# Attention and MoE block on one core: the layernorm's mean is subtracted from the data instead of from the output weights, scales are summed in one pass, and the list scheduler models the transfer queue

## The chip, the core and the metric

The kernel runs on one core of a Trainium2 chip. The metric is device time in microseconds; less is better. Every execution computes the whole result from tensors that lie in device memory. The profiler took one execution of the kernel before; all views quoted below are of that execution.

## What is computed

Eight batches of eight-head attention (576 tokens, head size 64), half of the heads with a local mask (the 32 latest keys), half with a strided mask (keys whose distance is a multiple of 32), then a feed-forward block over 4608 tokens:

```python
x = attention(q, k, v).transpose(0, 2, 1, 3).reshape(4608, 512)
h = x @ w_in                                  # 512 -> 1024
e = exp(h - max(h)); sm = e / (sum(e) + 1e-9)
solu = h * sm
mu = mean(solu); var = mean((solu - mu) ** 2)
ln = (solu - mu) / sqrt(var + 1e-6) * g_ln
out = ln @ w_out                              # 1024 -> 512
```

All tensors are float32, except that the two weight matrices are handed over as 64-bit numbers and decoded on the chip.

## The kernel before

**Precision by splitting.** [...] Each factor is scaled by a power of two and split into a high and a low half of 16 bits (`whi`/`wlo`, `xhi`/`xlo`, `c[:,0]`/`c[:,1]`, `ohi`/`olo`), and each product is three passes: high by high, high by low, low by high. The scales come from `pow2_scale`: a sum of squares over all partitions (on TensorE, line 254, a product with a matrix of ones, one 128x1 float32 product per column to add), whose exponent is halved on VectorE (L260 to L268).

**Attention.** A batch is five units (`UNITS`): two of the strided heads, three of the local heads. A unit runs query times key (L347 puts the mask into PSUM, L352 multiplies), the row maximum and the difference on VectorE (L358, L359), exp on ScalarE (L361), row sums (L362, L366, L367), the normalisation on GpSimd (L370), the 16-bit split (L376, L377), a transposing DMA (L379, tile `pt`), the product with the values (L400, into `x_ps`), and the split of the result into `xhi` and `xlo` (L416, L417). Before it `v_scale` and `v_split` (L289, L307, L308) prepare the values, and DMAs of L323 copy them into a second layout.

**Feed-forward.** 36 tiles of 128 tokens (`ff`, L421). The first product, here called g1, is two halves of 12 matrix products of 128x512 (L458 to L460), each half into one of three PSUM banks (`h_ps`). A tile uses two of them, so that the second half of the next tile has to wait until this tile's `h` was read for the last time (L469). Then, for a tile: maximum (L465) and its scaling (L466) on VectorE, exp with its sum (L467) on ScalarE, `u = h * e` with its sum (L469) and the mean (L472) on VectorE, the sum of squared deviations (L473) on ScalarE, six small instructions on GpSimd (L477 to L487) that end in the inverse root `r`, `c[:,0] = u * r` on ScalarE (L490), the low half `c[:,1]` on VectorE (L491), one transposing DMA (L494, tile `ct`, three buffers), the second product, here called g2 (24 products, L498 to L500), the scaling into `ob` on ScalarE (L506) and the store (L507). The mean itself is never subtracted from `u`: the mean over the rows of g times w_out is taken off the weights instead.

**Weights.** Both weight matrices are loaded in pieces of 128 rows and decoded (L522, L525, L528, L529). For `w_in`, ScalarE and TensorE make the two halves (L541, L547 to L557). For `w_out`, `prep_o` (L559) builds two gain matrices on GpSimd (L567, L570), sums the weighted rows on TensorE (L574, eight float32 products of 128x512) and squares on ScalarE (L562); `split_o` (L585) then forms, for each of the eight chunks, gain times weight minus the mean with two float32 products (L590, L591) in `x_ps`, and splits that (L594, L595). The two `x_ps` banks are those that the attention units use.

**What sets the order.** Nothing is ordered by hand. Each step is added to a `Plan` with an engine, an assumed duration, a key and the names that it reads and writes; `Plan.order` simulates the five engines with these durations, takes at each moment the ready step with the lowest key, and the instructions are then issued in that order. Each engine executes its own instructions strictly in this order. All loads, copies and transposes are issued by SyncE; the stores by ScalarE. In the plan a DMA takes 5 us beyond its turn in the queue (`DMA_LATENCY`), and SyncE may run 1 us ahead of it (`DMA_AHEAD`).

## Time and profile before

| what | value |
|---|---|
| runs | 567.52, 572.67, 572.97 us; median 572.67 |
| the profiled execution, first to last instruction | 566.9 us |
| lowest run less that span | 0.6 us |
| median less that span | 5.8 us |
| TensorE busy | 505.7 us, 89% of the span |
| VectorE, ScalarE, GpSimd busy | 355.9, 301.8, 156.7 us |
| mean granted TensorE clock | 0.985 |
| moved by DMA | 96.9 MB, mean 171 GB/s |

The profiled execution has no time of its own beside its span of 566.9 us; the sums of the prediction are made against that span, and the last step goes from it to the runs. Matrix products overlap, and each is shown with its full length: a product of 128x512 shows 0.38 us, but the next one starts 0.216 us later. What a step of TensorE costs is therefore read from the start of one step to the start of the next.

### The profile page before, as it was taken

To read this page: it belongs to the slowest core of one execution; us is meant where nothing else is said; L and a number is where in the kernel's file an instruction comes from. 1 tells how busy PE (TensorE), PEld (TensorE's weight loads), DVE (VectorE), ACT (ScalarE), POOL (GpSimd) and SP (SyncE) were. 2 spreads that over 40 slices of the span, in tenths; PEclk is the share of its full clock that TensorE was granted. 3 is DMA by queue.
4 is the path that set the end of the run, shared out by engine and by line. 5 is a ranking of instruction groups with operands and counts; after the bars stand their busy time and mean duration, and the time that the engine had idled before them with its cause. 6 is when DMAs were issued, how large, how long until landed. Compare 5 with 4: busy or idle time off the path is not lost.

```text
span 566.9 us, 11879 instructions
## 1 busy us (share of the span) xinstructions
PE 505.7 (89%) x4864; PEld 256.9 (45%) x4864; DVE 355.9 (63%) x633; ACT 301.8 (53%) x446; POOL 156.7 (28%) x309
## 2 busy tenths in 40 slices
PE   0348998999798999899999999999989999999986
PEld 0233444345453555455454554555545554444432
DVE  3596367867466775677766776877656777343430
ACT  3765824685256553755674556555744644345350
POOL 2320002433132342334331332322323323113130
PEclk9999978899999999999999999999999999999999
DMA  8999149629992999599938996899679635533332
GB/s 312 413 258 272 35 120 227 140 59 247 190 250 56 225 217 237 127 175 236 254 86 122 271 221 138 198 206 240 162 137 180 139 80 111 87 84 84 77 91 74
DMA packets 171158, 96.90 MB, mean 171 GB/s; under 512 B 138208, under 2 KB 157280, under 8 KB 171104
## 3 DMA queue, kind: packets, MB, share of 16 engines
q1 hardware_dynamic: 165920, 86.71, 70.8%
q10 hardware_dynamic: 5184, 9.44, 5.1%
q8 instruction: 38, 0.62, 0.5%
q14 instruction: 16, 0.13, 0.1%
HBM read 39.24 MB, written 9.44 MB: 86 GB/s over the span
## 4 chain that ended last, share of the span: by engine, by line
PE 72%; DVE 10%; DMA 9%; ACT 5%; issue 2%; POOL 1%; ACTq 0%; SPq 0%; DVEq 0%
PE h_ps L458 10%; PE h_ps L459 9%; PE h_ps L460 9%; PE o_ps L498 9%; PE o_ps L499 9%; PE o_ps L500 9%; PE x_ps L400 4%; PE s_ps L352 4%; DMA pt<-p 3%; DMA ct<-c 2%; DVE u L469 2%; DMA vrl<-vloc 2%; ACT e L467 2%; PE h_ps L553 2%; PE s_ps L347 1%
## 5 line engine op out<-in xcount | busy, mean ns | idle before, releaser
L458 PE MATMUL h_ps<-w,xhi 128*128 128x512 f16 x280 | 108.5, 388 | 10.5 <-DVE u L469 7.6
L459 PE MATMUL h_ps<-w,xhi 128*128 128x512 f16 x280 | 108.2, 386 | 0.0
L460 PE MATMUL h_ps<-w,xlo 128*128 128x512 f16 x280 | 107.7, 385 | 0.0
L498 PE MATMUL o_ps<-obuf,ct 128*128 128x512 f16 x272 | 103.4, 380 | 1.0 <-DMA ct<-c 0.8
L499 PE MATMUL o_ps<-obuf,ct 128*128 128x512 f16 x272 | 103.3, 380 | 0.0
L500 PE MATMUL o_ps<-obuf,ct 128*128 128x512 f16 x272 | 103.2, 379 | 0.0
L370 POOL TENSOR_TENSOR t<-t,m 128x576 f32<-128x576 f32 (+2 forms) x40 | 47.4, 1184 | 126.9 <-DVE m L367 101.1
L467 ACT ACTIVATE e<-h_ps,st,vsc 128x1024 f32<-128x1024 f32 x31 | 37.2, 1201 | 64.8 <-DVE st L466 49.4
L465 DVE TENSOR_REDUCE st<-h_ps 128x1 f32<-128x1024 f32 x35 | 42.6, 1218 | 41.9 <-PE h_ps L460 41.9
L477 POOL TENSOR_SCALAR st<-st 128x1 f32<-128x1 f32 x36 | 11.4, 316 | 208.3 <-DVE st L472 198.8
L469 DVE SCALAR_TENSOR_TENSOR u<-h_ps,e 128x1024 f32<-128x1024 f32 x35 | 42.8, 1222 | 29.1 <-ACT e L467 17.7
L473 ACT ACTIVATE e<-u,st 128x1024 f32<-128x1024 f32 x36 | 41.3, 1147 | 35.3 <-DVE st L472 32.1
L491 DVE SCALAR_TENSOR_TENSOR c<-u,st,c 128x1024 f16<-128x1024 f32 x36 | 47.0, 1304 | 14.6 <-ACT c L490 14.6
L417 DVE TENSOR_TENSOR xlo<-x_ps,xhi 128x384 f16<-128x384 f32 (+2 forms) x40 | 25.6, 641 | 40.4 <-ACT xhi L416 40.3
L490 ACT ACTIVATE c<-u,st 128x1024 f16<-128x1024 f32 x36 | 41.2, 1145 | 16.8 <-POOL st L487 16.0
L459 PEld LDWEIGHTS <-xhi 128*128 128x128 f16 x288 | 28.5, 99 | 40.2 <-issue 12.9
L498 PEld LDWEIGHTS <-ct 128*128 128x128 f16 x288 | 28.2, 98 | 39.4 <-DMA ct<-c 5.5
L458 PEld LDWEIGHTS <-xhi 128*128 128x128 f16 x288 | 28.8, 100 | 35.4 <-issue 5.9
L460 PEld LDWEIGHTS <-xlo 128*128 128x128 f16 x288 | 28.6, 99 | 35.4 <-issue 2.5
L500 PEld LDWEIGHTS <-ct 128*128 128x128 f16 x288 | 28.2, 98 | 34.2 <-issue 0.3
L499 PEld LDWEIGHTS <-ct 128*128 128x128 f16 x288 | 28.2, 98 | 32.3
L352 PE MATMUL s_ps<-k,q 64*54 64x54 f32 (+1 forms) x1280 | 41.8, 274 | 0.0
(143 smaller groups left out, 766.2 us busy)
## 6 DMA issues: line engine op xcount, KB each, us to landing
out<-ob ACTq DMA_DIRECT2D x36, 256.0 KB, 3.1
vrs<-vstr SPq DMA_DIRECT2D x8, 768.0 KB, 5.8
vd<-vs SPq DMA_DIRECT2D x16, 384.0 KB, 7.5
vrl<-vloc SPq DMA_DIRECT2D x8, 640.0 KB, 5.7
q<-qstr SPq DMA_DIRECT2D x8, 594.0 KB, 4.9
k<-kstr SPq DMA_DIRECT2D x8, 594.0 KB, 6.5
q<-qloc SPq DMA_DIRECT2D x8, 576.0 KB, 5.2
k<-kloc SPq DMA_DIRECT2D x8, 576.0 KB, 6.8
```

Of the source, the lines that this page charges most:

```text
L352: nc.tensor.matmul(s_ps[row : row + nq, pair, i * nk : (i + 1) * nk], q_raw[half][hs, q0 : q0 + (nq - 1) * nqb + 1 : nqb], k_raw[half][hs, ...
L370: add("pool", nx * nk / 500 + 0.1, lambda: nc.gpsimd.tensor_tensor(tv, tv, sm.unsqueeze(2).broadcast_to([P, nx, nk]), op=ALU.mult), key + ...
L458: nc.tensor.matmul(hv[:, i], xhi[:, cc, tok], whi[:, cc, cols], start=(cc == 0), stop=False)
L459: nc.tensor.matmul(hv[:, i], xhi[:, cc, tok], wlo[:, cc, cols], start=False, stop=False)
L460: nc.tensor.matmul(hv[:, i], xlo[:, cc, tok], whi[:, cc, cols], start=False, stop=(cc == 3))
L465: add("dve", 1.21, lambda: nc.vector.tensor_reduce(nm, hv, axis=AX.XY, op=ALU.max, negate=True), key + 0.2, r=HH, w=[(ST, "nm")])
L467: add("act", 1.3, lambda: nc.scalar.activation(ev, hv, AF.Exp, bias=nm, scale=hs, accum_out=z), key + 0.25, r=[*HH, (ST, "nm"), *SC], w=[E ...
L469: add("dve", 1.3, lambda: nc.vector.scalar_tensor_tensor(uv, hv, 1.0, ev, op0=ALU.mult, op1=ALU.mult, accum_out=us), key + 0.3, r=[*HH, E] ...
L491: add("dve", 1.35, lambda: nc.vector.scalar_tensor_tensor(c[:, 1], u, r, c[:, 0], op0=ALU.mult, op1=ALU.subtract), key + 0.45, r=[U, (ST, ...
L498: nc.tensor.matmul(o, ct[:, cc, :], ohi[:, cc, :], start=(cc == 0), stop=False)
L499: nc.tensor.matmul(o, ct[:, cc, :], olo[:, cc, :], start=False, stop=False)
L500: nc.tensor.matmul(o, ct[:, 8 + cc, :], ohi[:, cc, :], start=False, stop=(cc == 7))
```

## The change

1. **The mean.** The data is centred: ScalarE now makes `c[:,0] = u - mean` (with the mean as bias), VectorE the low half of it, and neither waits for the variance. The sum of squares (now into a scratch tile) comes after that, and GpSimd's five small instructions, which end in the factor `f` of the store, come last. The weights need no mean: `gmat`, `gdiag`, the eight products of L574, the sixteen of L590 and L591 and the copy `mt` are gone. `split_o` multiplies the decoded weight by gain times scale on ScalarE and takes the low half on VectorE, straight from SBUF; the decoded weights lie four chunks further up in `obuf`, so that the halves can be written below them.
2. **A range factor per tile.** Since `c` is no longer divided by the deviation, `u` is multiplied by a power of two `ia` that two small VectorE instructions (`span`) derive from the largest `h`; the scaling of the maximum is now three values wide.
3. **Scales.** `pow2_scale` adds its columns with one VectorE reduction into a 16-bit number and then runs one product with 16-bit ones, instead of one float32 product per column.
4. **The planner.** SyncE's transfers carry four numbers (how many queue entries, time to issue, delay until it begins, time to land), the queue is at most 100 entries deep, every landing is taken 3 us late, engines are free a little before a step ends, and most assumed durations are set anew. The base keys of the units, loads and tiles are unchanged.

The core of the diff, with long parts cut:

```diff
-    DMA_LATENCY = 5.0
-    DMA_AHEAD = 1.0
     HOP = 0.4
+    LATE = 3.0
+    DEEP = 100
+    SKIP = {"act": 0.1, "dve": 0.08, "pe": 0.07, "pool": -0.1}
...
-                dma_free = max(dma_free, now + 0.55) + dur
-                free[e] = max(now + 0.55, dma_free - self.DMA_AHEAD)
-                end = dma_free + self.DMA_LATENCY
+                pushes, issue, begins, lands = steps[n][6]
+                start = max(now + begins, dma_free)
+                dma_free = start + dur
+                pieces.append((start, dma_free, moved, moved + pushes))
+                moved += pushes
+                free[e] = now + issue + 0.06
+                for a, b, c, d in reversed(pieces):
+                    if c < moved - self.DEEP <= d:
+                        free[e] = max(free[e], a + (b - a) * (moved - self.DEEP - c) / (d - c))
+                        break
+                end = dma_free + lands + self.LATE
...
-        def total():
-            for i, part in enumerate(parts):
-                nc.tensor.matmul(tot, ones, part, start=(i == 0), stop=(i == len(parts) - 1))
+        def part_sum():
+            with nc.allow_low_precision(reason="a power of two is made of it"):
+                nc.vector.tensor_reduce(one, parts, axis=AX.X, op=ALU.add)
...
+        add("pe", 0.15, lambda: nc.tensor.matmul(tot, ones, one, start=True, stop=True), key, r=["ones", (w, "one")], w=[T])
...
+        def span():
+            nc.vector.tensor_scalar(near, up, floor, down, op0=ALU.max, op1=ALU.max)
+            nc.vector.tensor_scalar(ia.bitcast(I32), near.bitcast(I32), 0x7FFFFFFF, 0x7F800000, op0=ALU.bitwise_xor, op1=ALU.bitwise_and)
...
-        add("act", 1.35, lambda: nc.scalar.activation(e, u, AF.Square, bias=mean, scale=Q, accum_out=sq), key + 0.35,
-            r=[U, (ST, "mean")], w=[E, (ST, "sq")])
...
-        add("act", 1.2, lambda: nc.scalar.mul(c[:, 0], u, r), key + 0.4, r=[U, (ST, "r")], w=[(C, 0)])
-        add("dve", 1.35, lambda: nc.vector.scalar_tensor_tensor(c[:, 1], u, r, c[:, 0], op0=ALU.mult, op1=ALU.subtract), key + 0.45,
+        add("act", 1.2, lambda: nc.scalar.activation(c[:, 0], u, AF.Identity, bias=mean, scale=1.0), key + 0.35, r=[U, (ST, "mean")], w=[(C, 0)])
+        add("dve", 1.28, lambda: nc.vector.scalar_tensor_tensor(c[:, 1], u, mean, c[:, 0], op0=ALU.add, op1=ALU.subtract), key + 0.4,
...
+        add("act", 1.24, lambda: nc.scalar.activation(junk[:, 0:DF], u, AF.Square, bias=mean, scale=1.0, accum_out=sq), key + 0.42,
...
-        for cc in range(8):
-            add("pe", 0.87, lambda cc=cc: nc.tensor.matmul(o_ps, gmat[:, cc], obuf[:, cc], start=(cc == 0), stop=(cc == 7)), key,
-                r=["gmat", ("od", cc)], w=["o"])
...
-            def center(cc=cc, x=x):
-                nc.tensor.matmul(x, gdiag[:, cc], obuf[:, cc], start=True, stop=False)
-                nc.tensor.matmul(x, ones[0:1], mt_sb[0:1], start=False, stop=True)
...
+            add("act", 0.68, lambda cc=cc, go=go: nc.scalar.mul(ohi[:, cc], o32[:, cc], go), key, r=[("od", cc), "go"], w=[("oh", cc), *past])
```

What this does to the order shows at three places.

ScalarE near the end of the weight preparation, before: `ob` is the square of a `w_out` chunk, `xhi` the split of an attention unit, `junk` the squares of the next batch's values, and the `obuf` written from `x_ps` is the high half of a centred `w_out` chunk.

```order
L376 CAST p_97<-t_91 128x6x96
L562 ACTIVATE ob_113,o_sc_128<-obuf_126 128x512
L525 ACTIVATE obuf_126<-room_70 128x512
L562 ACTIVATE ob_113,o_sc_128<-obuf_126 128x512 x2
L416 CAST xhi_102<-x_ps 128x2x192
L525 ACTIVATE obuf_126<-room_67 128x512
L562 ACTIVATE ob_114,o_sc_128<-obuf_126 128x512 x2
L289 ACTIVATE junk_71,vm_79<-vrl_72 128x1280
L562 ACTIVATE ob_114,o_sc_128<-obuf_126 128x512
L289 ACTIVATE junk_71,vm_79<-vrs_73 128x1536
L583 COPY mt_122<-o_ps 128x512
L416 CAST xhi_102<-x_ps 128x2x192
```

And after the change, where `obuf` written from `obuf` with `gg` is the high half of a `w_out` chunk:

```order
L393 CAST p_99<-t_93 128x6x96
L584 ACTIVATE ob_116,o_sc_128<-obuf_126 128x512
L434 CAST xhi_104<-x_ps 128x2x18x18
L308 ACTIVATE junk_71,vm_79<-vrl_72 128x1280
L308 ACTIVATE junk_71,vm_79<-vrs_73 128x1536
L597 ACTIVATE obuf_126<-obuf_126,gg_131 128x512
L434 CAST xhi_104<-x_ps 128x2x18x15
L597 ACTIVATE obuf_126<-obuf_126,gg_131 128x512 x6
L434 CAST xhi_104<-x_ps 128x2x192
L597 ACTIVATE obuf_126<-obuf_126,gg_131 128x512
L323 ACTIVATE vs_75<-vrs_73,vsc_83 128x1536
L434 CAST xhi_104<-x_ps 128x2x192
```

The third split of the first batch (the first one of shape 128x2x192; the first tile needs three) stood before among the squares of `w_out`. It now stands behind all eight squares, the two `junk` squares of the next batch and seven high halves of `w_out`.

TensorE right after the first half of g1, before (`o_sc` and `vm` are the columns of squares):

```order
L400 MATMUL x_ps<-pt_101,vl_74 64x64
L254 MATMUL h_ps<-o_sc_128,ones_124 128x1 x8
L254 MATMUL s_ps<-vm_79,ones_124 128x1 x2
L590 MATMUL x_ps<-obuf_126,gdiag_120 128x512
L591 MATMUL x_ps<-mt_122,ones_124 128x512
L347 LDWEIGHTS unit_87
L347 MATMUL s_ps<-mk_loc_85,unit_87 64x288
```

And after:

```order
L418 LDWEIGHTS vl_74
L418 MATMUL x_ps<-pt_103,vl_74 64x64
L364 LDWEIGHTS unit_89
L364 MATMUL s_ps<-mk_loc_87,unit_89 64x288
L364 LDWEIGHTS unit_89
```

The sums and the first centring pair are gone from between the attention products; the two sums of one column each stand ahead of the first g1 now. Seven more pairs of L590 and L591 stood before the first g2, spread over the eight halves of g1 that came ahead of it. Now five halves of g1 come ahead of the first g2. From there on g1 and the g2 of an earlier tile mostly alternate by halves (12 products of the one, 12 of the other), where before g2 came by 24.

ScalarE in a late tile, before:

```order
L490 ACTIVATE c_109<-u_107,st_116 128x1024
L467 ACTIVATE e_104,st_117<-h_ps,st_117,vsc_83 128x1024
L473 ACTIVATE e_104,st_117<-u_106,st_117 128x1024
L506 ACTIVATE ob_113<-o_ps,st_115 128x512
L507 DMA out<-ob_113 128x512
L490 ACTIVATE c_108<-u_106,st_117 128x1024
```

And after:

```order
L494 ACTIVATE e_107,st_120<-h_ps,st_120 128x1024
L501 ACTIVATE c_111<-u_109,st_120 128x1024
L504 ACTIVATE junk_71,st_120<-u_109,st_120 128x1024
L494 ACTIVATE e_106,st_117<-h_ps,st_117,vsc_85 128x1024
L528 ACTIVATE ob_115<-o_ps,st_119 128x512
L529 DMA out<-ob_115 128x512
```

`e` is the exp, `c` the high half; L473 before and L504 after are the sum of squares, which has moved behind the high half.

More of the change, by code (lines that the diff above doesn't have):

```diff
@@ L99, in order @@
         ready_at = [0.0] * len(steps)
[L100 removed]
+        free = dict.fromkeys(("pe", "act", "dve", "pool", "sp"), 0.85)
         locked = dict.fromkeys(("dve", "pool"), 0.0)
[L102 removed]
+        dma_free, moved, pieces = 3.0, 0, []
         waiting = {e: [] for e in free}
@@ L128, in order @@
                     locked[e] = now + dur
-                free[e] = end = now + dur
+                end = now + dur
+                free[e] = end - (0.16 if dur > 2.4 else self.SKIP[e])
             for m in users[n]:
@@ L289, in square @@
                 nc.scalar.activation(junk[:, 0:w], vr_sb[a], AF.Square, scale=2.0**-SQ, accum_out=vm[:, a : a + 1])
-            add("act", (1.25, 1.47)[a], square, key, r=[("vr", a)], w=["junk", ("vm", b % 2, a)])
-        pow2_scale(sc, [vm[:, 0:1], vm[:, 1:2]], key, [("vm", b % 2, a) for a in range(2)], ("vsc", b % 4),
+            add("act", (1.36, 1.58)[a], square, key, r=[("vr", a)], w=["junk", ("vm", b % 2, a)])
+        pow2_scale(sc, vm[:, 0:2], vs1_sb[b % 2], key, [("vm", b % 2, a) for a in range(2)], ("vsc", b % 4),
                    (s_ps[:, 1, 511:512], ("s", 1)), 8, 1.0 / P_SCALE)
@@ L403, in unit @@
         VR = [("v2", half, i) for i in range(4 if half else 3)] + (["vz"] if half else []) + ([("v", 0, 0), ("v", 0, 1)] if half == 0 else [])
-        add("pe", nx * (0.063 if half else 0.095) + 0.1, pv, key + 0.9, r=[PT, *VR], w=X)
+        add("pe", nx * (0.06 if half else 0.1) + (0.22 if half else 0.16), pv, key + 0.9, r=[PT, *VR], w=X)
         off = (b % 2) * S
@@ L502, in ff @@
         for i in range(2):
-            add("pe", 2.6, lambda i=i: g2(i), key + G2LAG, r=[CT, *(("o_w", cc) for cc in range(4 * i, 4 * i + 4))], w=[O])
+            add("pe", 2.75, lambda i=i: g2(i), key + G2LAG, r=[CT, *(("o_w", cc) for cc in range(4 * i, 4 * i + 4))], w=[O])
         def store():
@@ L577, in comb @@
-        def comb():
-            nc.vector.tensor_tensor(o_sc[:, 8:16], o_sc[:, 8:16], g_sb, op=ALU.mult)
-            nc.vector.tensor_tensor(o_sc[:, 8:16], o_sc[:, 8:16], g_sb, op=ALU.mult)
-        add("dve", 0.48, comb, key, r=["g", *(("om", cc) for cc in range(8))], w=["om"])
-        pow2_scale(o_sc, [o_sc[:, 8 + cc : 9 + cc] for cc in range(8)], key, ["om"], "o_sc", (h_ps[:, 1, 0:1], ("h", 1)), square=2.0**10)
-        add("act", 0.62, lambda: nc.scalar.copy(mt_sb, o_ps), key, r=["o"], w=["mt"])
+        add("dve", 0.15, lambda: nc.vector.tensor_tensor(o_sc[:, 4:12], o_sc[:, 4:12], gg_sb[:, 0], op=ALU.mult), key,
+            r=["gg", *(("om", cc) for cc in range(8))], w=["om"])
@@ L585, in split_o @@
+        pow2_scale(o_sc, o_sc[:, 4:12], s1_sb[:, 1:2], key, ["om"], "o_sc", (h_ps[:, 1, 0:1], ("h", 1)))
+        add("dve", 0.15, lambda: nc.vector.tensor_scalar(gg_sb[:, 1], g_sb, o_sc[:, 1:2], None, op0=ALU.mult), key, r=["g", "o_sc"], w=["go"])
     def split_o(key):
         for cc in range(8):
-            x, X = x_ps[:, cc % 2], ("x", cc % 2)
-            def center(cc=cc, x=x):
-                nc.tensor.matmul(x, gdiag[:, cc], obuf[:, cc], start=True, stop=False)
-                nc.tensor.matmul(x, ones[0:1], mt_sb[0:1], start=False, stop=True)
@@ L599, in attn_solu_kernel @@
+            past = [("od", cc - OAHEAD)] if cc >= OAHEAD else []
+            add("act", 0.68, lambda cc=cc, go=go: nc.scalar.mul(ohi[:, cc], o32[:, cc], go), key, r=[("od", cc), "go"], w=[("oh", cc), *past])
+            add("dve", 0.7, lambda cc=cc, go=go: nc.vector.scalar_tensor_tensor(olo[:, cc], o32[:, cc], go, ohi[:, cc], op0=ALU.mult, op1=ALU.subtract), key,
+                r=[("oh", cc), ("od", cc), "go"], w=[("o_w", cc), *past], lock=True)
     load_qk(0, 1, LF[0])
```

199 lines of the change are left out of this document (98 added, 101 removed).

## The prediction

> **What bounds the kernel now.** First the page: PE's busy share and clock in 40 slices, in tenths.
>
> ```profile
> PE   0348998999798999899999999999989999999986
> PEclk9999978899999999999999999999999999999999
> ```
>
> TensorE (PE) does nothing in the first twentieth, is nearly always busy from a tenth of the span on, and has a low clock in slices 6 to 8. I cut the span at four events of the trace: the first product of g1 (66.4), the first of g2 (123.3), 200, and the last product of g1 (543.6). Columns: length, then busy time (and instructions) of PE, PEld, DVE, ACT, POOL; the clock; DMA share; GB/s.
>
> ```profile
> 0.00:66.40 66.40, 30.26 (x328) 17.48 (x329) 39.13 (x78) 41.59 (x71) 13.38 (x21) 1.00 0.92 275
> 66.40:123.30 56.90, 53.21 (x401) 24.45 (x399) 38.95 (x76) 29.07 (x45) 13.79 (x24) 0.88 0.59 135
> 123.30:200.00 76.70, 70.95 (x825) 37.88 (x824) 50.52 (x92) 40.43 (x59) 23.15 (x40) 0.98 0.87 184
> 200.00:543.60 343.60, 335.23 (x3251) 170.33 (x3244) 221.97 (x380) 185.04 (x267) 103.91 (x219) 1.00 0.77 160
> 543.60:566.90 23.30, 16.02 (x73) 6.74 (x71) 5.30 (x7) 5.63 (x8) 2.46 (x7) 1.00 0.33 79
> ```
>
> From 200 to 543.6 PE idles 8.4 of 343.6 us, from 123.3 to 200 5.8 of 76.7, while DVE has a third of its time free (221.97 of 343.6). So TensorE's work is the bound from 66.4 on: taking work from it there pays in full, and other engines matter by what they make it wait for. These are the waits, as total, count, longest:
>
> ```profile
> PE h_ps L458 <- DVE u L469: 7.6, 8, 2.7
> PE x_ps L400 <- DMA pt<-p: 3.0, 1, 3.0
> PE s_ps L498 <- DMA ct<-c: 3.5, 2, 1.9
> PE o_ps L498 <- DMA ct<-c: 0.8, 1, 0.8
> ```
>
> The third bank for g1 (7.6) and the transposes (3.0, and 3.5 at the end) are all that is worth naming. There is little left for a better order to win in the middle.
>
> **Term 1, the removed products.** Busy time of PE and PEld in the same stretches, for one line each: L590, L591, then L574, then L254 (three stretches).
>
> ```profile
> 66.40:123.30 56.90, 8.56 (x16) 2.79 (x16) 0.88 0.59 135
> 66.40:123.30 56.90, 9.83 (x16) 2.54 (x16) 0.88 0.59 135
> 0.00:66.40 66.40, 7.22 (x16) 2.91 (x16) 1.00 0.92 275
> 66.40:123.30 56.90, 2.39 (x20) 2.31 (x20) 0.88 0.59 135
> 123.30:200.00 76.70, 1.11 (x8) 1.12 (x8) 0.98 0.87 184
> 200.00:543.60 343.60, 2.11 (x16) 2.33 (x16) 1.00 0.77 160
> ```
>
> Between the first g1 and the first g2, 8.56 + 9.83 = 18.4 us are centring and 2.4 the sums. The idle time is 56.90 - 53.21 = 3.7. That leaves 32.4 us of g1 and attention, part of it at a low clock:
>
> ```profile
> 76.58 0.61 PE L458 MATMUL h_ps<-w,xhi 128*128 128x512 f16 x1
> 76.98 0.63 PE L459 MATMUL h_ps<-w,xhi 128*128 128x512 f16 x1
> 77.41 0.63 PE L460 MATMUL h_ps<-w,xlo 128*128 128x512 f16 x1
> 80.85 0.33 PE L347 MATMUL s_ps<-mk_str,unit 64*64 64x324 bf16 x4
> 84.40 0.39 PE L458 MATMUL h_ps<-w,xhi 128*128 128x512 f16 x1
> 87.09 0.31 PE L347 MATMUL s_ps<-mk_str,unit 64*64 64x270 bf16 x4
> ```
>
> One half of g1 took 4.27 us from its start to the next step (76.58 to 80.85), another 2.69 (84.40 to 87.09): a cold half costs 1.6 more. (Its products start 0.43 us apart, 76.98 to 77.41; twelve of those would make 5.1, so the clock came back within the half.) The stretch's clock of 0.88 is a loss of 0.12 x 56.9, some 6.8 us by that reading; three cold halves make 4.8, which I take. Useful work at full clock is then 32.4 - 4.8 = 27.6 us, and 8.5 us (3.7 + 4.8) were lost to waits and cold clock even with the centring there to fill gaps.
>
> **What waits in its place.** Without the centring, PE waits for the chain of the first tile: two readings of the tile chain, the last tile's, where nothing else runs, and one transpose in traffic.
>
> ```profile
> 543.77 1.24 DVE st L465
> 548.18 0.07 ACT e L473
> 550.95 1.16 ACT c L490
> 552.13 1.29 DVE c L491
> 553.48 4.24 DMA ct<-c
> 263.73 9.87 DMA ct<-c
> ```
>
> From the maximum to the landed transpose the undisturbed chain takes 543.77 to 557.72 = 13.95 us. The square and GpSimd's six instructions lie in it from 548.18 to 550.95; the change moves both behind the high half, so 2.77 us go and the chain is 11.2. In the ramp VectorE also serves the next batch's attention: the order puts 11 other VectorE instructions between the first tile's maximum and its low half. Seven are large, at the 0.75 us of a unit's instruction, and four small, at 0.2 (L358 and L466 below): about 6 us, so about 17. Behind the first tile's last half of g1 the order leaves TensorE three more halves (3 x 2.69) and attention steps of about 5 us, 13 in all, before it must wait for g2: 4 us of waiting. Add the third bank, 2.7 once or twice, and two cold halves (3.2): about 11 us of loss, against 8.5 before. Bounds: 5 (the centring hid nothing) to 20 (the transpose takes 9.87 instead of 4.24 and the bank is waited for at every tile).
>
> So the stretch becomes 27.6 + 11 = 38.6 instead of 56.9: **-18.3** (-24 to -9). The three halves that came before the first g2 and now come after it are in both counts, since they only change places with other work of TensorE.
>
> **Term 2, the start.** L574's 7.2 us stood ahead of the first g1 and go. But the first g1 also needs the third split of attention results, and the order moves that on ACT.
>
> ```profile
> 62.55 0.46 ACT L416 CAST xhi<-x_ps 128x384 f16<-128x384 f32 x1
> L562 ACT ACTIVATE ob<-obuf 128x512 bf16<-128x512 f32 x8 | 5.0, 631 | 0.1
> L594 ACT ACTIVATE obuf<-x_ps,o_sc 128x512 f16<-128x512 f32 x8 | 5.4, 680 | 8.7 <-PE x_ps L591 8.7
> L289 ACT ACTIVATE junk<-vrs 128x1536 bf16<-128x1536 f32 x8 | 11.8, 1477 | 0.1
> L289 ACT ACTIVATE junk<-vrl 128x1280 bf16<-128x1280 f32 x8 | 10.1, 1260 | 1.8 <-DMA vrl<-vloc 1.8
> 18.30:50.30 32.00, 16.84 (x224) 11.69 (x225) 25.57 (x48) 22.37 (x32) 8.17 (x5) 1.00 1.09 312
> ```
>
> Before, that split ended at 63.0. New ahead of it on ACT: four squares (0.63), two `junk` (1.48 + 1.26) and seven high halves (0.68): 2.5 + 2.7 + 4.8 = 10.0 us. Against it stands ACT's idle time from 18.3 to 50.3, 32.0 - 22.37 = 9.6 us, because the work that moved forward can fill it, where w_out has arrived in time. I take that half of it is recovered: 63.0 + 10.0 - 4.8 = 68.2, so the first g1 starts near 68 instead of 66.4: **+1.6**. Bounds 62 (all idle time recovered) and 73 (none).
>
> SyncE's first four transposes now stand behind the next batch's loads (q, k, both values) and w_out's last piece. Their takers, the first products with values, stand behind all of w_in's preparation on TensorE, which hides that; what it does not hide is in the upper bound of 73. GpSimd loses the two gain matrices, and the small instructions of a tile still wait there for the sum of squares as before, with the units' normalisations queued behind.
>
> **Term 3, small things.** The later sums (1.11 + 2.11 us) become eight products of one column; the trace has no 16-bit one, and the nearest row is L254's own, a quarter of a microsecond: at 0.1 each, 3.2 - 0.8 = **-2.4** (bounds -3.2 and 0, if the VectorE reduction ahead is waited for). Per tile VectorE gets two instructions more, and the pointer in `u`'s product:
>
> ```profile
> L466 DVE TENSOR_SCALAR st<-st,vsc 128x1 f32<-128x1 f32 x32 | 6.6, 206 | 0.5
> L358 DVE TENSOR_REDUCE m<-s_ps 128x6 f32<-128x576 f32 (+2 forms) x40 | 30.1, 752 | 13.3 <-PE s_ps L352 13.3
> L469 DVE SCALAR_TENSOR_TENSOR u<-h_ps,e 128x1024 f32<-128x1024 f32 x35 | 42.8, 1222 | 29.1 <-ACT e L467 17.7
> L491 DVE SCALAR_TENSOR_TENSOR c<-u,st,c 128x1024 f16<-128x1024 f32 x36 | 47.0, 1304 | 14.6 <-ACT c L490 14.6
> L595 DVE SCALAR_TENSOR_TENSOR obuf<-x_ps,o_sc,obuf 128x512 f16<-128x512 f32 x8 | 6.0, 746 | 2.5 <-ACT obuf L594 1.5 <-PE x_ps L400 0.8
> ```
>
> Two times 0.206 and some 0.08 (L491 with a pointer against L469 without one) make 0.5 us x 36 = 18 us of VectorE, which lie in the third of its time that is free: nothing; without that cover they would lengthen the wait for the bank, 0.5 for each tile. Its two instructions run beside the exp.
>
> **Term 4, the end.** Both waits of the last two g2 (3.5 together) are for the transpose. The chain is 2.77 shorter, and in the new order seven halves of g2 stand behind the last g1, 7 x 2.69 = 18.8 us, more than the chain of 11.2: **-3.5** (-3.5 to 0).
>
> **Term 5, the middle.** 5.8 + 8.4 = 14.2 us are idle. The shorter chain should reduce that; the new order brings g2 closer to its g1 (by my count of the products between them some 15 to 27 us of work instead of about 26), which should raise it. I take **0**, with bounds -8 (the waits for bank and transpose gone) and +15 (fifteen tiles wait another microsecond).
>
> Sum: 566.9 + 1.6 - 18.3 - 2.4 - 3.5 + 0 = 544.3 us of span. The runs lie 0.6 to 5.8 us above the profiled span. What makes the two slower runs is not in the profile; I add 1.7 and forecast **546 us**, 4.7% less than the median.
>
> **The clock.** The profile's clock falls to 0.7 in slice 6 (70.9 to 85.0), and a cold half costs 1.6 us. The Trainium skill, "TensorE: Matmul & The Clock Gate", Part 1, says that after an idle window of about 3.4 us the array runs at half its clock until it has been busy for another such window; the trace agrees, with products 0.43 us apart where they are else 0.216. It speaks against this change, which takes filler from TensorE.
>
> **The rivals.**
> - *VectorE bounds the ramp.* Its 38.95 us of work in 56.9 can't shrink as TensorE's does. In the long middle it reaches 65%; at 75%, with its 6.0 us of L595 gone ahead and 2 us added, (39 - 6 + 2) / 0.75 = 47 us: the stretch gains 10 instead of 18.3, so 554. For it: tile 0's chain shares VectorE with five units. Against it: TensorE still has three quarters of the stretch. 0.15.
> - *The ramp runs cold.* If all eight of its halves and two of g2 are cold, 10 x 1.6 = 16 instead of the 3.2 that I count, so 546 + 13 = 559. For it: PE idles before the first g1 more than before. Against: the cold half shown above was warm again before its end. 0.12.
> - *Slower: the new order waits at every g2.* Where two tiles instead of three are ahead, some 15 us of products cover a chain of 11.2 undisturbed, or 16.8 with a transpose of 9.87. If half of the tiles had the slow transpose and other work in front on ACT or DVE, 18 x 2.5 = 45 us come on top: 591. It is slower than before once those 18 wait 1.5 us each on top of today's. For it: transposes of 9.87 exist. Against: 3.5 + 0.8 us of waits for `ct` in the whole trace, and a planner that lands every transfer 3 us late. 0.05.
> - *The removal is not one:* the order has none of L574, L590, L591 left. 0.
>
> The forecast, with its bounds from 530 to 552, has 0.65; 0.03 is left for what I do not see. The range takes in the first two rivals: the low end is terms 1 and 2 at half of their better bounds and the middle's -8, 546 - 3 - 3 - 8 = 532, rounded to 530; the high end is the cold ramp, 560. A measurement of this kernel tells about 1% from no change. Faster by over 1%, below 567: the forecast and the first two rivals nearly whole, 0.90; within 1%: 0.05; slower: 0.05.
>
> **What will show it.** The first g1 between 62 and 73, and the first g2 within 45 us of it (term 1; over 50 means that VectorE or the cold clock took it). VectorE over 75% there speaks for the first rival, more 0.43 us gaps for the second. The waits of PE for `ct` should stay below 8 us; 30 or more is the third. No wait for `ct` behind the last g1 confirms term 4. I am wrong if the stretch shrinks by less than 9 us, or if the idle time of the middle grows past 29.

## The result, and the profile after

The changed kernel takes **585.85 us** (median of four runs, 583.66 to 589.82), the kernel before 570.2 (four runs, 567.52 to 572.97). The ratio is **1.029, 95% interval 1.021 to 1.037**: the change made the kernel slower, where 546 us and a chance of 0.9 for faster stood in the prediction. The profiled execution took 589.82 us, the longest of the four and 1.7 more than its span of 588.1; all views of the changed kernel are of that one.

The page of the changed kernel: PE's busy share in 40 slices, and its clock.

```profile
PE   0147476979999899789799887989989999999966
PEclk9998698889999999789799999989989999999999
```

Before, the row of PE was nearly all 9s and 8s from a tenth of the span on, and the clock was low in one place. Now both dip all through the middle. The windows of the changed kernel, cut at the first product of g1 (69.3), the first of g2 (101.8), the first g2 of the second tile (125.6), 200 and the end of g1 (559.4); the columns are those of the prediction's table.

```profile
0.00:69.30 69.30, 22.65 (x304) 13.29 (x304) 43.77 (x91) 47.94 (x82) 9.34 (x31) 0.93 0.89 264
69.30:101.80 32.50, 23.93 (x313) 12.89 (x314) 25.15 (x51) 13.51 (x19) 6.30 (x9) 0.87 0.86 171
101.80:125.60 23.80, 19.78 (x184) 8.88 (x184) 15.05 (x23) 9.67 (x14) 5.44 (x12) 0.82 0.67 142
125.60:200.00 74.40, 73.79 (x709) 36.73 (x704) 49.91 (x94) 41.66 (x61) 17.64 (x35) 1.00 0.74 161
200.00:559.40 359.40, 331.66 (x3183) 165.09 (x3181) 232.55 (x437) 178.70 (x258) 85.47 (x148) 0.96 0.74 153
559.40:588.10 28.70, 19.43 (x88) 8.33 (x86) 7.76 (x13) 8.90 (x14) 5.50 (x13) 1.00 0.40 92
```

From 200 us to the end of g1 PE idles 359.40 - 331.66 = 27.7 us, where it was 8.4. Cut at 200 us alone, the two kernels stand like this (length, then PE's busy time; before first, the changed kernel second):

```profile
0.00:200.00 200.00, 154.42 (x1552) 79.82 (x1552) 128.61 (x246) 111.08 (x173) 50.32 (x84) 0.96 0.81 200
200.00:566.90 366.90, 351.25 (x3322) 177.07 (x3314) 227.27 (x387) 190.67 (x275) 106.38 (x226) 1.00 0.74 155
```

```profile
0.00:200.00 200.00, 140.15 (x1503) 71.79 (x1504) 133.88 (x256) 112.78 (x175) 38.71 (x86) 0.93 0.80 196
200.00:588.10 388.10, 351.09 (x3269) 173.42 (x3266) 240.31 (x449) 187.59 (x271) 90.98 (x161) 0.96 0.71 149
```

In the first 200 us, 29.1 us of products were removed (8.56 + 9.83 + 7.22 + 2.39 + 1.11 in the prediction's rows), and PE is busy 14.3 us less. The other 14.8 are work done sooner, less about 2 us of further cold products: at 200 us the changed kernel is some 13 us ahead. The rest should then take 366.9 - 12.8 - 2.1 (the later sums) = 352 us. It takes 388.1. Of these 36 us, 21.3 are idle time (37.0 instead of 15.7), and 14.8 lie in a PE that is slower while it is busy.

What PE waits for from 200 to 559.4, as total, count, longest (the six largest of eight rows):

```profile
PE s_ps L364 <- DVE t L376: 6.5, 2, 3.4
PE x_ps L418 <- DVE xlo L435: 5.8, 3, 2.8
PE h_ps L476 <- DVE u L497: 4.4, 4, 1.6
PE h_ps L476 <- ACT e L494: 3.9, 5, 2.2
PE o_ps L520 <- DMA ct<-c: 2.7, 1, 2.7
PE s_ps L277 <- DVE vs L274: 1.9, 2, 1.6
```

The transpose ahead of g2 is waited for once. More than half of the 27.7 us is **attention**: the next unit's scores wait until VectorE has read the last ones (6.5), the products with values wait for the low halves (5.8), a batch's sum of squares for its columns (1.9). In the same stretch before, all waits of attention's steps made 1.7 us. And what follows such a wait runs cold:

```profile
240.30 0.61 PE L520 MATMUL o_ps<-obuf,ct 128*128 128x512 f16 x1 [2.71 <-DMA ct<-c]
240.70 0.63 PE L521 MATMUL o_ps<-obuf,ct 128*128 128x512 f16 x1
...
365.40 0.32 PE L364 MATMUL s_ps<-mk_loc,unit 64*64 64x288 bf16 x4 [3.38 <-DVE t L376]
365.52 0.86 PE L369 MATMUL s_ps<-k,q 64*64 64x96 f32 x24
366.32 0.61 PE L520 MATMUL o_ps<-obuf,ct 128*128 128x512 f16 x1
366.72 0.63 PE L521 MATMUL o_ps<-obuf,ct 128*128 128x512 f16 x1
```

The products start 0.40 us apart instead of 0.216. Six halves of g1 and g2 after 200 us take 4.29 to 4.93 us from start to end instead of 2.75, 10.4 us together, and before there was none. That is most of the 14.8. The clock record of the trace agrees: from 200 us on it has eight windows of 3.41 us at half the clock, in which PE was busy for 23.5 us and so lost 11.7; before it has none there. About 3 us stay without an account.

### The profile page after: what moved, and what is told of

It reads as the page before. It is cut to its first block, busy times and chain, and to the rows that moved or that the text cites. A ratio compares the mean times of both kernels' runs of the same rounds, so it can differ in the third digit from the quotient of the medians.

```text
span 588.1 us, 11772 instructions
## 1 busy us (share of the span) xinstructions
PE 491.2 (84%) x4770; PEld 245.2 (42%) x4770; DVE 374.2 (64%) x705; ACT 300.4 (51%) x445; POOL 129.7 (22%) x247
## 4 chain that ended last, share of the span: by engine, by line
PE 64%; DVE 16%; DMA 10%; ACT 4%; issue 4%; SPq 1%; ACTq 0%; DVEq 0%
PE h_ps L476 10%; PE h_ps L478 10%; PE h_ps L477 10%; PE o_ps L520 8%; PE o_ps L521 7%; PE o_ps L522 7%; DVE st L483 4%; DMA ct<-c 4%; PE x_ps L418 4%; PE s_ps L369 3%; DVE u L497 3%; DMA room<-w_in 2%; PE h_ps L574 2%; ACT e L494 2%; DVE c L502 2%
## 5 line engine op out<-in xcount | busy, mean ns | idle before, releaser
L476 PE MATMUL h_ps<-w,xhi 128*128 128x512 f16 x280 | 110.4, 394 | 19.8 <-DVE u L497 11.7
L520 PE MATMUL o_ps<-obuf,ct 128*128 128x512 f16 x272 | 106.9, 393 | 7.7 <-DMA ct<-c 5.6
L478 PE MATMUL h_ps<-w,xlo 128*128 128x512 f16 x280 | 110.0, 393 | 0.3 <-DVE xlo L435 0.3
L477 PE MATMUL h_ps<-w,xhi 128*128 128x512 f16 x280 | 110.1, 393 | 0.0
L521 PE MATMUL o_ps<-obuf,ct 128*128 128x512 f16 x272 | 106.1, 390 | 0.0
L522 PE MATMUL o_ps<-obuf,ct 128*128 128x512 f16 x272 | 105.7, 388 | 0.0
L387 POOL TENSOR_TENSOR t<-t,m 128x576 f32<-128x576 f32 (+2 forms) x40 | 48.6, 1214 | 172.1 <-DVE m L384 108.6
L497 DVE SCALAR_TENSOR_TENSOR u<-h_ps,st,e 128x1024 f32<-128x1024 f32 x35 | 44.7, 1278 | 48.5 <-PE h_ps L478 26.6
L502 DVE SCALAR_TENSOR_TENSOR c<-u,st,c 128x1024 f16<-128x1024 f32 x36 | 50.0, 1389 | 21.8 <-ACT c L501 21.6
L378 ACT ACTIVATE t<-t 128x576 f32<-128x576 f32 (+2 forms) x40 | 27.5, 687 | 50.6 <-DVE t L376 50.2
L510 POOL TENSOR_SCALAR st<-st 128x1 f32<-128x1 f32 x36 | 20.2, 561 | 140.0 <-ACT junk L504 139.3
L477 PEld LDWEIGHTS <-xhi 128*128 128x128 f16 x288 | 28.9, 100 | 50.6 <-issue 22.1
L520 PEld LDWEIGHTS <-ct 128*128 128x128 f16 x288 | 28.7, 100 | 46.2 <-DMA ct<-c 11.2
L522 PEld LDWEIGHTS <-ct 128*128 128x128 f16 x288 | 28.9, 100 | 36.2 <-issue 3.8
L521 PEld LDWEIGHTS <-ct 128*128 128x128 f16 x288 | 28.9, 100 | 31.6 <-issue 4.4
L504 ACT ACTIVATE junk<-u,st 128x1024 bf16<-128x1024 f32 x36 | 40.9, 1137 | 2.1 <-ACT ob L528 2.1
```

The costliest lines, as they stand in the source:

```text
L387: add("pool", nx * nk / 510 + 0.02, lambda: nc.gpsimd.tensor_tensor(tv, tv, sm.unsqueeze(2).broadcast_to([P, nx, nk]), op=ALU.mult), key + ...
L476: nc.tensor.matmul(hv[:, i], xhi[:, cc, tok], whi[:, cc, cols], start=(cc == 0), stop=False)
L477: nc.tensor.matmul(hv[:, i], xhi[:, cc, tok], wlo[:, cc, cols], start=False, stop=False)
L478: nc.tensor.matmul(hv[:, i], xlo[:, cc, tok], whi[:, cc, cols], start=False, stop=(cc == 3))
L497: add("dve", 1.3, lambda: nc.vector.scalar_tensor_tensor(uv, hv, ia, ev, op0=ALU.mult, op1=ALU.mult, accum_out=us), key + 0.3, r=[*HH, E, ...
L502: add("dve", 1.28, lambda: nc.vector.scalar_tensor_tensor(c[:, 1], u, mean, c[:, 0], op0=ALU.add, op1=ALU.subtract), key + 0.4, r=[U, (ST, ...
```

## Experiments

Each kernel ran beside the kernel before on the same chip; the ratio is to that. "Idle" is PE's idle time in the profile, ahead of 200 us and from 200 us to the end (length less busy time of such windows as above). Before has 45.6 and 15.7, the changed kernel 59.9 and 37.0.

| run | what | us | ratio, 95% interval | idle to 200, from 200 |
|---|---|---|---|---|
| e1_path_only | new arithmetic, old planner | 599.98 | 1.051 (1.046 to 1.056) | 60.0, 50.5 |
| e2_order_only | old arithmetic, new planner | 584.45 | 1.023 (1.020 to 1.026) | 42.3, 24.2 |
| e3_old_queue | changed kernel, old transfer figures | 583.82 | 1.022 (1.016 to 1.027) | 65.4, 30.1 |
| e4_late6 | changed kernel, transfers 6 us late | 600.12 | 1.049 (1.046 to 1.053) | 62.6, 41.6 |
| e5_g2_behind | changed kernel, g2's key later | 565.94 | 0.994 (0.991 to 0.997) | 62.2, 21.9 |
| e6_keys_refit | and other keys | 560.44 | 0.984 (0.977 to 0.991) | 59.1, 16.3 |
| e7_before_g2_behind | before, g2's key later | 568.88 | 0.998 (0.994 to 1.002) | 41.8, 17.2 |
| e8_tk0 | changed kernel, tiles' keys earlier | 563.95 | 0.992 (0.989 to 0.996) | 60.0, 20.6 |
| e10_free_scratch | changed kernel, scratch freed | 571.36 | 1.003 (1.001 to 1.005) | 64.2, 23.5 |
| e12_free_g2 | and g2's key later | 547.88 | 0.962 (0.957 to 0.966) | 61.4, 7.3 |
| e14_free_refit | and all keys set anew | 541.53 | 0.951 (0.948 to 0.955) | 58.3, 6.6 |
| e15_before_junk | before, scratch shared | 602.47 | 1.059 (1.054 to 1.063) | 45.6, 37.5 |
| e16_old_list | new arithmetic in before's list | 565.91 | 0.994 (0.991 to 0.998) | 65.4, 16.2 |
| e13_path_free | e1 with the scratch freed | 574.24 | 1.006 (1.002 to 1.010) | 61.0, 28.9 |
| e17_before_refit | e2 with all keys set anew | 563.23 | 0.988 (0.982 to 0.993) | 39.7, 12.4 |

### First question: the arithmetic or the order?

**e1_path_only**: the changed kernel, with before's planner.

```diff
 class Plan:
-    LATE = 3.0
-    DEEP = 100
-    SKIP = {"act": 0.1, "dve": 0.08, "pe": 0.07, "pool": -0.1}
+    DMA_LATENCY = 5.0
+    DMA_AHEAD = 1.0
...
-            add("pe", 2.75, lambda i=i: g1(i), key, ...
+            add("pe", 2.6, lambda i=i: g1(i), key, ...
```

> The changed arithmetic (mean off the data, single-pass sums) ordered by the planner of before: its class, its durations of the steps that both kernels have, its two figures for the transfer queue. Theory S, the new list order costs the time (PE idles 27.7 us from 200 to 559.4 in the changed kernel, 8.4 in the same stretch of before): the arithmetic alone takes some 29 us of products away, so 548 to 555. Theory D, the arithmetic itself costs it (VectorE 374.2 us instead of 355.9, and two instructions more between maximum and product on the engine that frees TensorE's banks): no better than the changed kernel, 578 to 592.

Measured 599.98 us, slower than the changed kernel and outside both ranges. So theory S fails as put: the new order is not what costs the time of the new arithmetic, since the old planner serves it worse. Theory D has the direction, but not the size.

**e2_order_only**: before, with the changed kernel's planner and durations.

```diff
 class Plan:
-    DMA_LATENCY = 5.0
-    DMA_AHEAD = 1.0
+    LATE = 3.0
+    DEEP = 100
+    SKIP = {"act": 0.1, "dve": 0.08, "pe": 0.07, "pool": -0.1}
```

> The arithmetic of before, ordered by the planner of the changed kernel (its class with the transfer queue, its durations). Theory S: the idle time of the middle comes with the order, some 20 to 35 us more than before: 588 to 605. Theory D: the order is harmless or helps a little: 562 to 573.

Measured 584.45 us, between the two ranges. Theory D fails as well: without any new arithmetic the new planner costs 13 us. Either half of the change alone makes the kernel slower, and the two together are no worse than the cheaper half. That does not look like two costs that add up; it looks like lists that are sensitive to something in common.

**e3_old_queue** and **e4_late6**: two changes of the transfer model.

```diff
...
-                end = dma_free + lands + self.LATE
+                dma_free = max(dma_free, now + 0.55) + dur
+                free[e] = max(now + 0.55, dma_free - 1.0)
+                end = dma_free + 5.0
...
```

> The changed kernel, whose planner has its new durations for the engines but the transfer figures of before (a transfer occupies the queue for longer and lands 5 us behind; SyncE is kept until 1 us before the end). Theory S in its narrow form, the model of the transfer queue is what puts transposes and loads into bursts: 550 to 565. If the new durations of the engines make the order, or theory D holds: 578 to 592.

```diff
-    LATE = 3.0
+    LATE = 6.0
```

> The changed kernel with one figure of its planner altered: every transfer is taken to land 6 us late instead of 3, since transposes of 8 to 12 us stand in the trace. If the order is too sure of its transfers: 560 to 575. If the waits are VectorE's own (PE's longest in the middle are for the units' subtraction and the low halves), under theories S or D: 580 to 592.

583.82 and 600.12 us, the second outside both of its ranges: the old queue figures change nothing, and a planner that is more careful about transfers makes a worse list. The model of the queue is not the cause.

### Second question: the priorities

The base keys were left as they were, while the tile's chain became shorter. Theory K says that they no longer fit.

```diff
-G2LAG = 0.55
+G2LAG = 3.35
```

> The changed kernel with one figure altered: the priority of g2 stands 3.35 behind that of its tile's g1 instead of 0.55, so that TensorE takes g2 only when nothing of the next three tiles is ready; in the order 31 us of products then lie between a tile's g1 and its g2, instead of 22 in the changed kernel and 26 in before. Theory K, the priorities were fitted to the longer chain of before, and with the shorter one g2 goes ahead of the next g1 and of the units, so that TensorE starts late what VectorE and ScalarE need next, and later waits for them: 548 to 565, with the idle time of the middle (27.7 from 200 to 559.4) halved. Theory D, VectorE's longer work for a tile costs the time, wherever g2 stands: 578 to 592.

Measured 565.94 us, 0.9 above what K expected: one figure is worth 20 us, and theory D is out, since VectorE's work is the same. From 200 us on idle time falls from 37.0 to 21.9, and the clock record has no low window left there.

**e6_keys_refit** moves other keys too (chosen, like those of the two refits below, for the shortest list in the planner's own reckoning):

```diff
-TK = [1.11 * t + 1.0 for t in range(NT)]
-G2LAG = 0.55
-KX = 0.5
-VK = [-25.0, *(5.0 * b - 8.0 for b in range(1, B))]
+TK = [1.11 * t - 0.9 for t in range(NT)]
+G2LAG = 3.35
+KX = -1.3
+VK = [-23.0, *(5.0 * b - 9.5 for b in range(1, B))]
...
```

> As the run with g2 behind, and five other priorities moved too: the tiles 1.9 earlier, the split of an attention result 1.8 earlier, the values 1.5 earlier, loads and weights by 0.2 to 2. Theory K: at least as fast as with g2 alone, 542 to 560. Theory D: 575 to 592.

560.44 us, 0.4 above what K expected. The control, the same figure in the kernel before:

```diff
-G2LAG = 0.55
+G2LAG = 3.35
```

> The control: before with the same figure, 3.35 instead of 0.55 (35 us of products between g1 and g2 instead of 26). Theory K: before's priorities fit its chain, so nothing to win, 565 to 578. If a later g2 is a gain by itself, whatever the chain: 550 to 562.

568.88 us, no change: a later g2 is no gain by itself. And another key of the changed kernel:

```diff
-TK = [1.11 * t + 1.0 for t in range(NT)]
+TK = [1.11 * t + 0.0 for t in range(NT)]
```

> The changed kernel with every priority of a tile one unit earlier against those of attention (the line of TK has + 0.0 instead of + 1.0), g2 still 0.55 behind g1. Theory K: another fit of the same figures, better by luck or not, 555 to 585. Theory D: 578 to 592.

563.95 us. K holds, but it is not the whole matter: here g2 follows its g1 after 22 us of products, as in the changed kernel, and the time falls just as far. So "g2 too early" was not the mechanism, or not the only one. What the shift of the tiles' keys does instead stays open.

### Third question: what keeps attention from running ahead

What the runs of the new arithmetic up to here have in common is where attention stands. Tile 7 (counted from 0) needs attention's tenth unit. Its low half on VectorE and the first product of the tile's g1, before first, the changed kernel second:

```profile
156.60 0.56 DVE L417 TENSOR_TENSOR xlo<-x_ps,xhi 128x384 f16<-128x384 f32 x1 [2.80 <-ACT xhi L416]
...
185.32 0.38 PE L458 MATMUL h_ps<-w,xhi 128*128 128x512 f16 x1
```

```profile
168.92 0.55 DVE L435 TENSOR_TENSOR xlo<-x_ps,xhi 128x384 f16<-128x384 f32 x1
...
169.86 0.39 PE L476 MATMUL h_ps<-w,xhi 128*128 128x512 f16 x1
```

Before, attention was done 28 us ahead; now 0.4 us. Counted like this for all tiles from the eighth to the thirty-first, before had 1 to 4 further units finished when a tile's g1 began; the changed kernel had none for 14 of the 24 tiles, 1 or 2 for nine, and for one the last unit was not quite finished when the first products started. The start of a batch's attention is the squares of its values on ScalarE, `junk`. Those of the fourth batch, and the square of tile 8, before and then the changed kernel:

```profile
174.88 1.26 ACT L289 ACTIVATE junk<-vrl 128x1280 bf16<-128x1280 f32 x1
...
213.58 1.14 ACT L473 ACTIVATE e<-u,st 128x1024 f32<-128x1024 f32 x1
```

```profile
196.88 1.15 ACT L504 ACTIVATE junk<-u,st 128x1024 bf16<-128x1024 f32 x1
197.93 0.19 ACT L504 ACTIVATION_READ_ACCUMULATOR junk<-u,st 128x1 f32 x1
198.15 1.27 ACT L308 ACTIVATE junk<-vrl 128x1280 bf16<-128x1280 f32 x1
```

Here is the cause of the lost lead. In the kernel before the tile's square wrote its unread result into `e`. The change writes it into `junk`, where the values' squares write theirs. Nobody reads either. But the planner knows names only: two steps that write `junk` keep the order in which the program adds them, and the program adds the values of batch b + 1 behind the tiles that batch b - 1 completes. So the next values may not be touched until that last tile has come as far as its square. First square of the values less the square of that tile, us:

| batch | 2 | 3 | 4 | 5 | 6 | 7 |
|---|---|---|---|---|---|---|
| before | -10.9 | -38.7 | -38.3 | -46.8 | -33.7 | -47.0 |
| changed | +1.3 | +1.3 | +1.3 | +1.3 | +1.3 | +1.3 |

Six times 1.3 us, the length of a square and its accumulator read. Theory J: this is what costs. Two opposite tests, in which no instruction differs, only the list.

**e10_free_scratch**: the changed kernel, with one name less.

```diff
-            r=[U, (ST, "mean")], w=["junk", (ST, "sq")])
+            r=[U, (ST, "mean")], w=[(ST, "sq")])
```

> The changed kernel with one word less in its planner's list: the tile's square no longer names the scratch tile junk among what it writes. The instructions are the same ones, with the same operands (ScalarE runs both users of junk itself, one after the other); only their order differs. Theory J: the scratch, which the changed kernel shares between the tile's square and the squares of the values, makes the planner put the next values' squares behind the square of the last tile of two batches before, so attention can't run ahead of the tiles; in before it ran 2 or 3 units ahead, in the changed kernel 0 or 1. Without the word the lead is back, PE's idle time from the 200th us on falls from 27.7 to about 10 and the cold products go: 547 to 560. Theory K alone (the priorities misfit, the scratch is harmless): 575 to 592.

**e15_before_junk**: the kernel before, with one name more.

```diff
-            r=[U, (ST, "mean")], w=[E, (ST, "sq")])
+            r=[U, (ST, "mean")], w=[E, "junk", (ST, "sq")])
```

> The reverse: before, whose planner is told that the tile's square writes junk too (one word more in the list; the instructions are the same). Theory J: attention loses its lead here as well, 583 to 605. Theory K alone: before's priorities fit before's chain, 565 to 578.

The reverse is as J expected: 602.47 us, 34 us slower than before, for a word that changes nothing on the chip but the order. The rows of tile 8 and the fourth batch in it:

```profile
208.80 1.15 ACT L473 ACTIVATE e<-u,st 128x1024 f32<-128x1024 f32 x1 [3.43 <-DVE st L472]
...
209.95 1.25 ACT L289 ACTIVATE junk<-vrl 128x1280 bf16<-128x1280 f32 x1
```

All six batches now follow their tile after 1.1 to 1.2 us, and PE's idle time from 200 us on goes from 15.7 to 37.5, that of the changed kernel. Freeing the scratch in the changed kernel brought 571.36 us: J is right in kind (14 us gained, the values' squares 20 to 48 us ahead of the tile's again, one low clock window from 200 us on instead of eight), but it missed its range of 547 to 560. What is left shows in the waits of this run from 200 to 530:

```profile
PE h_ps L476 <- DVE u L497: 7.9, 5, 2.7
PE h_ps L476 <- DVE st L483: 4.1, 6, 1.2
PE h_ps L476 <- ACT e L494: 2.4, 5, 1.2
PE s_ps L277 <- DVE vs L274: 1.4, 1, 1.4
```

Attention's waits are gone but for 1.4 us for a sum of squares and 0.3 for a scale. Now g1 waits for its banks, 14.4 us. That is the other half, and K's part. **e12_free_g2** has both.

```diff
-G2LAG = 0.55
+G2LAG = 3.35
...
-            r=[U, (ST, "mean")], w=["junk", (ST, "sq")])
+            r=[U, (ST, "mean")], w=[(ST, "sq")])
```

> As the run with the scratch freed, and g2's priority 3.35 behind g1's instead of 0.55. Theory J with K as a second, smaller part: 540 to 553, below the run with the scratch alone. If the late g2 only made up for the missing lead: no better than the scratch alone, 550 to 560.

547.88 us. All waits that PE has from 200 to 530 in this run:

```profile
PE h_ps L476 <- ACT e L494: 2.0, 5, 0.6
PE h_ps L476 <- DVE u L497: 1.4, 1, 1.4
```

The waits for banks fell from 14.4 to 3.4. With the low priority, g2 stays in reserve and stands between two tiles' g1 while VectorE reads the banks; with 0.55 it is taken as soon as the plan lands its transpose, and nothing is left to put there. That reading of the mechanism is argued from these two lists of waits; the time of the key, 23 us, is measured.

The lead alone does not set the time, though. In e5, e6 and e8 the name is still shared, the values' squares follow the tile's by 1.3 to 2.2 us, and of the same 24 tiles 18, 18 and 13 begin with no further unit finished, and two more in each run before their own last unit is: no better than in the changed kernel. Yet attention's waits from 200 to 530 us are 2.6, 3.1 and 3.9 us there against 15.0, and these runs are 20 to 25 us faster. And e2 lost 13 us with the lead intact (its squares stand 12 to 52 us ahead). So the 15 us of attention's waits need both, the shared name and the keys of the changed kernel. Freeing the name is worth 14 us with those keys, 18 with g2's key later (e5 to e12), 26 under the old planner (e1 to e13 below).

**e14_free_refit**: the scratch freed, and all keys set anew.

```diff
-TK = [1.11 * t + 1.0 for t in range(NT)]
-G2LAG = 0.55
-KX = 0.5
+TK = [1.13 * t - 0.4 for t in range(NT)]
+G2LAG = 3.75
+KX = -0.2
...
-            r=[U, (ST, "mean")], w=["junk", (ST, "sq")])
+            r=[U, (ST, "mean")], w=[(ST, "sq")])
```

> As the run with the scratch freed, with all priorities set anew (g2 3.75 behind, tiles 1.4 earlier at the start, values, loads and weights moved by 0.5 to 2.5). 538 to 552 if the priorities of before still cost something; 550 to 560 if not.

**541.53 us**, 4.9% below the kernel before (interval 4.5 to 5.2%), the best of all runs of either arithmetic. PE's busy slices and clock on its page:

```profile
PE   0136487989997999999999999999999999999997
PEclk9999777999999999999999999999999999999999
```

From 200 to 540 PE idles 6.6 us, and no slice after the seventh has a low clock.

### Fourth question: is the arithmetic worth it?

**e16_old_list** runs the new arithmetic in before's list, step by step, without a planner.

```diff
-    for n in plan.order():
+    for n in BEFORE_ORDER:
         plan.steps[n][2]()
```

> The changed arithmetic in the very order of before: no planner, but before's list step by step, with the centring products and the two gain matrices left out, the tile's square and the first half of its split in each other's places on ScalarE, and the new small steps where their inputs are ready. 26 us of products lie between g1 and g2, attention runs 2 or 3 units ahead. If the loss is the order's alone, this is what the prediction forecast: 543 to 556. If the arithmetic costs time in any order: 560 to 575.

565.91 us, in the range of the second forecast, and 4 us below the kernel before. But that forecast's reason, a cost in any order, does not hold: e12 and e14 have the same arithmetic and take 548 and 542. The windows (first g1 at 61.2, first g2 at 116.8) say where the 29 us went here:

```profile
61.20:116.80 55.60, 36.05 (x351) 17.74 (x352) 39.86 (x82) 32.34 (x50) 13.99 (x17) 0.82 0.60 138
116.80:200.00 83.20, 78.03 (x929) 40.70 (x928) 57.97 (x109) 43.12 (x62) 25.14 (x34) 0.96 0.90 189
200.00:542.00 342.00, 332.88 (x3142) 167.20 (x3141) 232.70 (x438) 182.30 (x264) 89.80 (x162) 1.00 0.74 157
```

From 200 us on it idles as little as before (9.1 us against 8.4). But the ramp from the first g1 to the first g2 is 55.6 us long, as it was (56.9), with 18.4 us of centring less in it: 19.6 us of PE's time there are idle, against 3.7. So in this list the centring had been filler nearly whole. In all kernels with the new arithmetic PE idles 58 to 65 us ahead of 200 us, against 45.6; at the 14 us that the changed kernel adds there, the removal of 29.1 us pays half.

**e13_path_free**: e1 with the scratch freed.

```diff
-            r=[U, (ST, "mean")], w=["junk", (ST, "sq")])
+            r=[U, (ST, "mean")], w=[(ST, "sq")])
```

> The changed arithmetic by before's planner, durations and priorities, with the scratch freed (the run with the arithmetic alone took 600 with the scratch shared). If the scratch was all that was wrong there: 543 to 556. If the priorities misfit the shorter chain under this planner too: 560 to 580.

574.24 us, 26 less than with the scratch shared. So J's cost is there under the old planner too. That the keys are what is left there is argued: no run sets them anew under that planner.

**e17_before_refit**: e2 with keys set anew for the old arithmetic.

```diff
-TK = [1.11 * t + 1.0 for t in range(NT)]
-G2LAG = 0.55
-KX = 0.5
+TK = [1.11 * t - 0.5 for t in range(NT)]
+G2LAG = 5.05
+KX = 2.5
...
```

> The arithmetic of before by the changed kernel's planner, with all priorities set anew for it (g2 5.05 behind g1). The run with that planner and the old priorities took 584. It has the 29 us of products that the change takes away. If the order of before is close to the best that its arithmetic allows: 560 to 570, some 20 above the best run of the changed arithmetic. If a refit order hides the centring: 545 to 555, and the changed arithmetic is worth 5 to 10.

563.23 us, 21 less than with the old keys and 22 above the best of the new arithmetic. With keys set anew by the same reckoning on both sides the new arithmetic is worth 22 us (21 by the ratios of 0.988 and 0.951); no run shows that either set of keys is the best. That this lies near the 22.6 of span that the prediction gave it is luck in part: ahead of 200 us e14 idles 18.6 us more than e17, where the forecast had 12.9 more than before, and it makes the difference up later (6.6 us of idle time against 12.4).

## Why the prediction was wrong, point by point

- **Term 5, the middle, is the step that failed.** It stood at 0 with bounds of -8 and +15. Measured: 21.3 us more of idle time from 200 us to the end, and a PE some 15 us slower while busy, 10.4 of them six cold halves. Counted as the prediction counted it, from the first g2 to the end of g1, idle time went from 14.2 to 32.4, past the 29 that it had named as a sign of being wrong. It asked how far g2 stands behind its g1, the place where the chain ends, and priced only that. Nothing in it looked at attention, where more than half of the middle's new waits lie. The edit without which they go (the square's result now goes to `junk`; e10 has 1.7 us of them left) appears in the text as "into a scratch tile" and was costed at nothing, without naming who else writes there. Its trace was in the order: the values' squares stood right behind a tile's square.
- **Term 5's second half**, that a shorter chain takes idle time away and an earlier g2 gives some back, had the right signs and too small a second one: the key of g2 alone is worth 20 us here, and 23 with the scratch freed. That the distance from g1 to g2 is what costs is not shown, since e8 gains as much at the same distance. The bound of "another microsecond for fifteen tiles" missed that such a wait is often followed by a cold half.
- **Terms 1 and 2, ramp and start, held about.** The first g1 came at 69.3 (forecast 68, 62 to 73), the first g2 32.5 us later (within 45). The 38.6 of the forecast held eight halves of g1 and the 32.5 hold five; with three more at 2.69 it is 40.6. (PE was not idle in the whole first twentieth of the span before: its second slice stands at three tenths. Nothing rests on it.) Counted at 200 us, the gain is 13 us where these terms and the early sums gave 17.8. Idle time ahead of 200 us rose by 14.3; the forecast had 8.8 for the start and 4.1 for the ramp.
- **Term 3, small things.** VectorE's share from 200 us to the end of g1 is 232.55 of 359.4, 65% as before, so its new instructions did find free time; e16 has them too and idles as little as before there. The products of the sums took 0.17 us each instead of 0.1, and from 200 us on PE waited 1.9 us for the reduction ahead of them, which is the case that the bound of 0 stood for.
- **Term 4, the end, did not come.** The end of g1 to the end of the span took 28.7 us (23.3 before). Two waits ahead of g2 were forecast to go; one of 2.6 us for a transpose is left, and two for `ob` of line 528, 2.9 together, are new.
- **The rivals.** "The new order waits at every g2" had the right sign and, by chance, nearly the time (591), but not the mechanism: the transpose is waited for once in the middle, 2.7 us, and 8.2 us in the whole trace (2.9 ahead of the first g2, 2.6 at the end), a hair over the 8 that the prediction allowed and far from 30. The cold ramp did not decide (the clock was 0.87 and 0.82, against 0.88 before). VectorE was busy 77% of the stretch to the first g2, over the 75% that was to speak for it, but the stretch was short all the same.
- **The clock.** The sentence that the removed filler speaks against the change was right in direction: 10 us of cold products. It was put to the ramp, and they came in the middle. That the trace agrees holds for the half rate only. The cold half quoted there followed no idle window: the clock fell at 73.0 us, and from 62.1 to 76.6 PE shows no wait. In the window ahead of that fall it ran attention's products, 20 of one column (L254) and the first of L590; which of these lets the clock fall is not shown.

## What to carry to other kernels

When a planner orders by names, a scratch tile is a name: ask of each new write who else writes there, and look in the order for steps that now stand back to back on that engine. When a chain gets shorter, the keys that were set around the old one have to be set again before the change is judged; here the freed name and the new keys together were the difference between +2.9% and -4.9%, and the new keys of e6 without the freed name gave -1.6%. The planner's own total, worked out from each list without the chip, ranks these: 568.6 us for the changed kernel against 553.2 for the old arithmetic by the same planner (e2), 548.1 with the name freed (e10), 523.7 for e14. It is no forecast of times: e8 and e2 stand at 552.9 and 553.2 there and took 564 and 584. And work that is removed from a stretch with waits in it pays only what is not filled by the waits, here half.

## What the runs showed of the hardware

TensorE's clock fell after shorter waits than expected. The Trainium skill, "TensorE: Matmul & The Clock Gate", Part 1, speaks of an idle window of about 3.4 us that runs free. In the 17 profiles of this case, counted from 130 us on, all 11 idle times of PE over 3.4 us were followed within 8 us by at least three products of g1 or g2 that start 0.36 to 0.6 us apart; so were 18 of 24 between 2.7 and 3.4 us, 8 of 20 between 2.0 and 2.7, and 14 of 61 between 1.4 and 2.0. A wait under 3.4 us can therefore cost a cold half of 1.6 us on top.

What decides most cases can be read from the clock records. In each of the 17 profiles the clock changes only at whole multiples of 3.41 us from its other changes, on a grid whose place differs from profile to profile, and it is either full or half. The idle time of PE that falls into one such window sorts the cases better than the length of the wait. From 130 us on, of the windows at full clock the next one ran at half after all 42 with over 2.03 us idle, after 16 of 59 with 1.43 to 2.03, and after none of 2011 with less. So it matters where a wait lies: in e10 one of 2.71 us fell into two windows, 1.78 and 0.93, and the clock stayed full. These figures hold for the mix of products from 130 us on; at 73.0 us in the kernel before the clock fell after a window with no idle time.
